# Two layers, forward and backward: the norm backward's last sum moved to VectorE, gradient copies halved, tail loads spread

## The chip, the cores and the metric

The kernel runs on one core of a Trainium2 chip. The metric is the device time of one execution in microseconds (us). Time before: 1142.19 us, the median of 3 runs (1139.85 to 1144.12).

The core's engines have the names that the profile gives them: PE is TensorE (matmul; PEld its weight load), DVE is VectorE, ACT is ScalarE, POOL is GpSimd, SP is SyncE, which here only issues transfers. "L860" is line 860 of the kernel file.

## The reference

Four residual layers are applied to x of 2048 x 512 in turn, attention (A), gated unit (B), A, B, with the same weights for both A and both B. The kernel returns the output and the gradients with respect to x and to all weights.

```python
def _layernorm(x, axis=-1, eps=1e-5):
    m = jnp.mean(x, axis=axis, keepdims=True)
    v = jnp.var(x, axis=axis, keepdims=True)
    return (x - m) / jnp.sqrt(v + eps)
# A: linear attention, 32 heads of 16
qkv = x @ wqkv                                    # 512 x 1536
pq, pk = phi(q), phi(k)                           # phi(t) = t+1 for t > 0, else exp(t)
kv, z = einsum(pk, v), sum(pk)
o = (pq @ kv) / (pq @ z)
A(x) = o @ wo                                     # 512 x 512
# B: F = 1376
B(x) = (sigmoid(x @ w_gate) * (x @ w_up)) @ w_down
# ... (cut: masks, shapes, small constants)
x = x + A(_layernorm(x)); x = x + B(_layernorm(x))
x = x + A(_layernorm(x)); x = x + B(_layernorm(x))
# outputs: x, and the vjp of it with grad_out for x, wqkv, wo, w_gate, w_up, w_down
```

The layers are numbered 0 (A), 1 (B), 2 (A), 3 (B). The backward goes 3, 2, 1, 0. Products are bfloat16, sums float32. The tokens are 16 tiles of 128 rows, in 4 blocks of 4 tiles (NB = 4, NBLK = 4); F is cut into 11 chunks of 128 (NFC = 11).

## The kernel before

Layer 3 is done forward and backward together; then `backward` runs layer 2 (`a_bwd`), layer 1 (`b_bwd`), layer 0 (`a_bwd`), and after these the gradients of the weights, for which activations and gradients that were stored before are loaded again, the latter transposed by the transfer.

Every tile of every layer goes through the backward of the norm. Its last line has two forms: one DVE operation, where `k.n_t` is 2 (layer 3), or a bias pass on ACT and a sum on POOL (layers 2, 1 and 0, where `k.n_t` is 4):

```python
def ln_bwd(k, l, st, dh_ps, h_st, up):
    nc = k.nc
    rstd = k.rstd[l][:, st:st + 1]
    c1 = k.small.tile([P, 1], F32, name="c1")
    c2 = k.small.tile([P, 1], F32, name="c2")
    t_sb = k.p_ln.tile([P, D], F32, name="t_sb", bufs=k.n_t)
    nc.scalar.activation(t_sb[:], dh_ps, ACT.Identity, scale=rstd, accum_out=c1[:])
    c1n = k.small.tile([P, 1], F32, name="c1n")
    nc.scalar.mul(c1n[:], c1[:], -1.0 / D)
    junk = k.p_ln.tile([P, D], BF16, name="junk", bufs=1)
    nc.vector.scalar_tensor_tensor(junk[:], t_sb[:], -1.0 / D, h_st, ALU.mult, ALU.mult, accum_out=c2[:])
    nc.vector.scalar_tensor_tensor(t_sb[:], h_st, c2[:], t_sb[:], ALU.mult, ALU.add)
    if k.n_t == 2:
        nc.vector.scalar_tensor_tensor(k.xs[st][:], t_sb[:], c1n[:], up, ALU.add, ALU.add)
    else:
        nc.scalar.activation(t_sb[:], t_sb[:], ACT.Identity, bias=c1n[:])
        nc.gpsimd.tensor_tensor(k.xs[st][:], t_sb[:], up, ALU.add)
```

Layer 1. A chunk is 4 matmuls into `dhh_ps`, a copy on ACT, a product `dd_t` on DVE, and 8 matmuls (`back`) that wait for `dd_t` and are queued two chunks later. At the end of a block, `back` starts the norm for four tiles:

```python
# ... (cut: b_bwd: pools with 4 buffers for dd_t, 2 for dhh_t)
        def back(b, fc, dd):

            if fc == 0:
                acc[b] = [k.ps2.tile([P, D], F32, name="dh_ps", tag="dwbank") for _ in range(NB)]
            for j in range(NB):
                for a in range(2):
                    nc.tensor.matmul(acc[b][j][:], lhsT=dd[:, a, rows(j)], rhs=(k.wuT, k.wgT)[a][:, fc, :],
                                     start=(fc == 0 and a == 0), stop=(fc == NFC - 1 and a == 1))
            if fc == NFC - 1:
                hst = k.p_h.tile([P, NB, D], BF16, name="hb_t", tag="h_t")
                nc.sync.dma_start(out=hst[:], in_=by_tile(sv["h"], b * NB, NB))
                for j in range(NB):
                    ln_bwd(k, l, b * NB + j, acc[b][j][:], hst[:, j, :], k.xs[b * NB + j][:])
# ... (cut: the sh_t loads)
            for f0, nf in FGRP:
                # ... (cut)
                for fc in range(f0, f0 + nf):
                    i = fc - f0
                    ps = k.ps.tile([P, SB], F32, name="dhh_ps", tag="bank")
                    mm4(k, ps[:], lambda c: k.wdT[:, c, FC0[fc]:FC0[fc] + P], lambda c: gTs[b][:, :, c, :])
                    dhh = p_g.tile([P, SB], BF16, name="dhh_t")
                    nc.scalar.mul(dhh[:], ps[:], 0.5)
                    dd = p_dd.tile([P, 2, SB], BF16, name="dd_t")
                    nc.vector.tensor_tensor(dd[:], dhh[:].unsqueeze(1).to_broadcast([P, 2, SB]), sh[:, i],
                                            ALU.mult)
                    late.append((b, fc, dd))
                    if fc < 4 if b == 0 else fc < 3:
                        k.fill.step(5 if b == 0 else 3)
                    store_dd(k, sv, b, fc, dd, nc.sync)
                    if len(late) > 2:
                        back(*late.pop(0))
                    if fc == 3 and b + 1 < NBLK:
                        grads(b + 1)
        while late:
            back(*late.pop(0))
```

Layers 2 and 0, first half. A block has four chunks dc; `a_grads` makes the bfloat16 copies of the next block's gradients (ACT), transposes them (PE) and copies these out of PSUM (ACT), all four tiles at chunk 1. `k.fill.step(n)` queues n matmuls of layer 3's w_down gradient, which have no other hurry. `soft` is queued two chunks late:

```python
def a_grads(k, b):
    nc = k.nc
    g_t = k.p_h.tile([P, NB, D], BF16, name="ga_t", tag="h_t")
    gT = k.p_hT.tile([P, NB, NDC, P], BF16, name="gaT_t", tag="hT_t")
    for j in range(NB):
        nc.scalar.copy(g_t[:, j, :], k.xs[b * NB + j][:])
        if j % 2 == 0:
            tp = k.ps.tile([P, 2 * NDC, P], BF16, name="T_ps", tag="bank")
        for c in range(NDC):
            nc.tensor.transpose(tp[:, j % 2 * NDC + c, :], g_t[:, j, c * P:(c + 1) * P], k.ident[:])
        if j % 2:
            nc.scalar.copy(gT[:, j - 1:j + 1].rearrange("p a c q -> p (a c) q"), tp[:])
    return g_t, gT
# ... (cut)
    grads = lambda b: gs.append(a_grads(k, b))

# ... (cut: sums: 16 matmuls into CT_ps)
    def soft(b, dc, dq, u_t, qp, rp, dqT):
        t_ps = k.ps.tile([P, SB], F32, name="t_ps", tag="bank")
        nc.tensor.matmul(t_ps[:], lhsT=k.bdmask[:], rhs=u_t[:], start=True, stop=True)
        w_t = ph1.tile([P, SB], BF16, name="w_t")
        nc.vector.scalar_tensor_tensor(w_t[:], t_ps[:], A["nz"][:, dc:dc + 1], dq[:], ALU.mult, ALU.add)
        nc.gpsimd.tensor_tensor(dqT[:, dc, :], w_t[:], rp[:, dc, :], ALU.mult)
        nc.vector.scalar_tensor_tensor(u_t[:], t_ps[:], -1.0, qp[:, dc, :], ALU.mult, ALU.mult,
                                       accum_out=dzp[:, dc, b:b + 1])
# ... (cut: loads of qr_l and qn_l for each block)
        for dc in range(NDC):
            ps = k.ps.tile([P, SB], F32, name="dq_ps", tag="bank")
            mm4(k, ps[:], lambda c: MT[:, c, dc * P:(dc + 1) * P], lambda c: gT[:, :, c, :])
            dq = ph1.tile([P, SB], BF16, name="dq_sb", bufs=3)
            k.mark = nc.scalar.copy(dq[:], ps[:])
            u_t = ph1.tile([P, SB], BF16, name="u_t", bufs=3)
            nc.vector.tensor_tensor(u_t[:], dq[:], qp[:, dc, :], ALU.mult)
            late.append((b, dc, dq, u_t, qp, rp, dqT))
            k.fill.step(2)
            if len(late) > 2:
                soft(*late.pop(0))
            if dc == 1 and b + 1 < NBLK:
                grads(b + 1)
        sums(b, g_t, qn)
```

Second half of these layers: `keys` writes `dkT_t` with DVE for the next block, from 16 matmuls in four PSUM banks `dpk_ps`; then 48 matmuls into `dh_ps`, and the norm's backward for the four tiles of the block.

The weight gradients. `joint(i, a)` is a job of 128 matmuls (`dw_cols`), a third of the columns of w_up or w_gate, over both B layers. `load_all` brings one stored tensor whole into SBUF, 4 transfers of 512 KB; its pool `dw_all` has two buffers, and `h2`, `h0` take those of `h3`, `h1`. `pieces` brings the other operand in parts of 4 tiles, most of them transposed by the transfer, through 6 buffers (`set_t`). All these transfers are issued by SP.

```python
        h3, h1 = load_all(k, sv[3]["h"], "h_all"), load_all(k, sv[1]["h"], "h_all")
        joint = lambda i, a: dw_cols(k, ("wu", "wg")[a], 0, SETS[i],
                                     [(h3, sv[3]["ddT"][a], sv[3]["ddN"][:, :, :, a]), (h1, sv[1]["ddT"][a])])
        k.p_dst = mpool("dw_stage", 6)
        joint(0, 0)
        mctx.close()
        k.p_set, k.p_dst = pool("dw_set_end", 6), pool("dw_stage_end", 6)
        k.p_sm = pool("dw_small", 2)
        for i, a in ((0, 1), (1, 0), (1, 1), (2, 0), (2, 1)):
            joint(i, a)
        p_all, k.p_all = k.p_all, pool("dw_all_end", 2)
        g1 = load_all(k, sv[1]["g"], "g_all")
        k.p_all = p_all
        h2, h0 = load_all(k, sv[2]["h"], "h_all"), load_all(k, sv[0]["h"], "h_all")
        for s in SETS:
            dw_rows(k, "wd", s, [(g1, sv[1]["hhT"])], sv[3]["wd"])
        for i, nm in ((1, "dkT"), (0, "dqT")):
            dw_cols(k, "wqkv", i * D, (0, D), [(h2, sv[2][nm]), (h0, sv[0][nm])])
            if i:
                dw_small(k)
```

```python
def put(k, ps, nm, rs, cs):

    r, w = ps.shape[0], ps.shape[1]
    new = k.p_dst.tile([P, D], BF16, name="dw_new")
    k.nc.scalar.copy(new[0:r, 0:w], ps)
    k.st.dma_start(out=k.outs[nm][rs, cs], in_=new[0:r, 0:w])
# ... (cut)
def dw_cols(k, nm, base, cols, srcs):

    c0, w = cols
    ps = dw_banks(k, NDC)
    for i, (h, src, *turned) in enumerate(srcs):
        for st, h_t, t in pieces(k, h, src, c0, w, *turned):
            for ic in range(NDC):
                k.nc.tensor.matmul(ps[ic][:, 0:w], lhsT=h_t[:, ic * P:(ic + 1) * P], rhs=t,
                                   start=(i == 0 and st == 0), stop=(i == len(srcs) - 1 and st == NST - 1))
    for ic in range(NDC):
        put(k, ps[ic][:, 0:w], nm, rows(ic), slice(base + c0, base + c0 + w))
# ... (cut: dw_rows, the same with g_all, adding the stored part of layer 3: part_l, L1203; sum on DVE, L1205)
```

## Time and profile before

| | us |
|---|---|
| time, median of 3 runs | 1142.19 (1139.85 to 1144.12) |
| profiled execution: span | 1140.3 |
| layer 2 backward | 525 to 643 |
| layer 1 backward | 643 to 769 |
| layer 0 backward, first half | 769 to 820 |
| layer 0 backward, second half | 820 to 890 |
| weight gradients | 890 to 1140 |

One line of a group in the page reads: line, engine, operation, out<-in, partitions x elements, count | busy us, mean ns of one | idle time of the engine just before them, and who ended most of it. Groups that the change touches:

```profile
L860 POOL TENSOR_TENSOR x<-t_sb,x 128x512 f32<-128x512 f32 x48 | 74.1, 1558 | 139.7 <-ACT c1n L852 115.8
L902 DVE TENSOR_TENSOR dd_t<-dhh_t,sh_t 128x1024 bf16<-128x1024 bf16 x44 | 33.7, 771 | 59.9 <-ACT dhh_t L900 54.5
L1185 PE MATMUL dw_ps<-set_t,h_all 128*128 128x512 bf16 (+1 forms) x1024 | 204.8, 362 | 1.4 <-ACT dw_new L1117 1.3
L1117 ACT CAST dw_new<-dw_ps 128x512 bf16<-128x512 f32 (+1 forms) x40 | 19.7, 573 | 219.8 <-PE dw_ps L1185 155.8
```

Matmuls are pipelined: 379 ns is the latency of one, and they start 0.216 us apart. A row of waits reads: engine, line, waited for whom: us in total, times, longest. A timeline row reads: start, duration, engine, line, operation, tiles, form, how many in a row, and the idle time before with who ended it.

### The profile page before, as it was taken

The numbers are of one execution on the slowest core, as the hardware profiler recorded it, in microseconds if no ns is written. First come the engines' busy times: TensorE is split into PE (matmuls) and PEld (weight loads), VectorE is DVE, ScalarE is ACT, GpSimd is POOL, SyncE is SP. The second block draws the span as 40 slices with busy tenths as digits, with TensorE's granted clock in tenths as the row PEclk, the third lists the DMA queues.
The fourth block names the chain that finished last, engine by engine and source line by source line (L and its number), as shares of the span: only waits on it lengthen the run. The fifth ranks groups of instructions, "written<-read, shape, count | busy, mean of one in ns | idle before, by whom it ended". The sixth has DMA issues, their size and how long they took to land.

```text
span 1140.3 us, 15748 instructions
## 1 busy us (share of the span) xinstructions
PE 1082.1 (95%) x5624; PEld 509.3 (45%) x5624; DVE 533.9 (47%) x951; ACT 506.8 (44%) x1034; POOL 381.7 (33%) x463
## 2 busy tenths in 40 slices
...
GB/s 258 256 235 239 264 244 244 182 181 245 285 231 106 236 78 250 89 266 247 271 282 212 191 232 247 219 182 308 336 182 95 191 275 172 136 216 250 228 231 115
DMA packets 376175, 248.13 MB, mean 218 GB/s; under 512 B 288784, under 2 KB 340528, under 8 KB 374304
## 3 DMA queue, kind: packets, MB, share of 16 engines
...
q8 instruction: 44, 0.72, 0.3%
...
## 4 chain that ended last, share of the span: by engine, by line
PE 20%; issue 20%; POOL 4%; DVE 4%; ACT 3%; DMA 3%; SPq 1%; POOLq 0%; DVEq 0%; ACTq 0%
PE dh_ps L879 5%; PE dhh_ps L180 2%; DVE junk L854 2%; PE fill_ps L236 2%; PE CT_ps L966 2%; POOL out_dram L1118 2%; PE dh_ps L790 2%; POOL x L860 2%; PE dh_ps L1037 2%; PE dq_ps L180 2%; DVE t_sb L855 1%; PE dh_ps L1098 1%; DMA qr_l<-sv_qr 1%; DMA pkT_l<-sv_pkT 1%; ACT t_sb L850 1%
## 5 line engine op out<-in xcount | busy, mean ns | idle before, releaser
L1185 PE MATMUL dw_ps<-set_t,h_all 128*128 128x512 bf16 (+1 forms) x1024 | 204.8, 362 | 1.4 <-ACT dw_new L1117 1.3
L651 POOL TENSOR_TENSOR sd_t<-sd_t,hh_t 128x512 bf16<-128x512 bf16 x88 | 107.8, 1236 | 121.6 <-DVE hh_t L649 89.2
L1185 PEld LDWEIGHTS <-h_all 128*128 128x128 bf16 x1024 | 100.2, 98 | 105.3 <-issue 1.9
L860 POOL TENSOR_TENSOR x<-t_sb,x 128x512 f32<-128x512 f32 x48 | 74.1, 1558 | 139.7 <-ACT c1n L852 115.8
L1117 ACT CAST dw_new<-dw_ps 128x512 bf16<-128x512 f32 (+1 forms) x40 | 19.7, 573 | 219.8 <-PE dw_ps L1185 155.8
L850 ACT ACTIVATE t_sb<-dh_ps,rstd 128x512 f32<-128x512 f32 x64 | 43.5, 680 | 127.7 <-PE dh_ps L790 93.4
L180 PE MATMUL g_ps<-hT_t,wg 128*128 128x512 bf16 x352 | 90.5, 379 | 6.9 <-DVE hh_t L649 3.7
L180 PE MATMUL u_ps<-hT_t,wu 128*128 128x512 bf16 x352 | 90.9, 380 | 0.6 <-DVE hh_t L649 0.6
L180 PE MATMUL dhh_ps<-gT_t,wdT 128*128 128x512 bf16 x352 | 91.2, 382 | 0.0
L1205 DVE TENSOR_TENSOR dw_new<-dw_ps,part_l 128x512 bf16<-128x512 f32 (+1 forms) x11 | 6.9, 684 | 179.7 <-PE dw_ps L1199 171.3
L1118 POOL DMA_DIRECT2D out_dram<-dw_new x40 | 21.4, 541 | 171.7 <-ACT dw_new L1117 170.3
L879 PE MATMUL dh_ps<-wuT,dd_t 128*128 128x512 bf16 x176 | 66.7, 379 | 3.8 <-DVE dd_t L902 3.7
L879 PE MATMUL dh_ps<-wgT,dd_t 128*128 128x512 bf16 x176 | 66.7, 379 | 0.0
L649 DVE SCALAR_TENSOR_TENSOR hh_t<-sd_t,u_ps 128x512 bf16<-128x512 bf16 x88 | 59.3, 679 | 14.1 <-ACT sd_t L648 13.5
L648 ACT ACTIVATE sd_t<-g_ps,onef 128x512 bf16<-128x512 f32 x88 | 60.8, 691 | 2.5
L902 DVE TENSOR_TENSOR dd_t<-dhh_t,sh_t 128x1024 bf16<-128x1024 bf16 x44 | 33.7, 771 | 59.9 <-ACT dhh_t L900 54.5
L650 ACT ACTIVATE sd_t<-g_ps,onef 128x512 bf16<-128x512 f32 x88 | 60.6, 689 | 0.0
L733 DVE TENSOR_TENSOR sd_t<-dhh_t,sd_t 128x1024 bf16<-128x1024 bf16 x44 | 30.4, 692 | 59.2 <-POOL sd_t L651 57.8
L647 ACT ACTIVATE g_ps<-g_ps 128x512 f32<-128x512 f32 x88 | 52.4, 602 | 8.8 <-PE g_ps L180 8.6
L180 PEld LDWEIGHTS <-wg 128*128 128x128 bf16 x352 | 33.9, 98 | 47.1 <-issue 8.8
L879 PEld LDWEIGHTS <-dd_t 128*128 128x128 bf16 x352 | 34.1, 98 | 46.4 <-DVE dd_t L902 5.8
L180 PEld LDWEIGHTS <-wu 128*128 128x128 bf16 x352 | 34.5, 98 | 42.3 <-issue 0.9
...
## 6 DMA issues: line engine op xcount, KB each, us to landing
...
```

The source lines that it names most:

```text
L180: i = k.nc.tensor.matmul(out, lhsT=lhs(c), rhs=rhs(c), start=(c == 0), stop=(c == n - 1))
L647: nc.scalar.activation(g_ps[:], g_ps[:], ACT.Tanh, scale=-0.5)
L648: nc.scalar.activation(sd[:, 0, :], g_ps[:], ACT.Identity, bias=k.onef[:], scale=-1.0)
L649: nc.vector.scalar_tensor_tensor(hh[:], sd[:, 0, :], 0.5, u_ps[:], ALU.mult, ALU.mult)
L650: nc.scalar.activation(sd[:, 1, :], g_ps[:], ACT.Identity, bias=k.onef[:])
L651: nc.gpsimd.tensor_tensor(sd[:, 1, :], sd[:, 1, :], hh[:], ALU.mult)
L850: nc.scalar.activation(t_sb[:], dh_ps, ACT.Identity, scale=rstd, accum_out=c1[:])
L860: nc.gpsimd.tensor_tensor(k.xs[st][:], t_sb[:], up, ALU.add)
L879: nc.tensor.matmul(acc[b][j][:], lhsT=dd[:, a, rows(j)], rhs=(k.wuT, k.wgT)[a][:, fc, :], start=(fc == 0 and a == 0), stop=(fc == NFC - 1 ...
L902: nc.vector.tensor_tensor(dd[:], dhh[:].unsqueeze(1).to_broadcast([P, 2, SB]), sh[:, i], ALU.mult)
L1118: k.st.dma_start(out=k.outs[nm][rs, cs], in_=new[0:r, 0:w])
L1185: k.nc.tensor.matmul(ps[ic][:, 0:w], lhsT=h_t[:, ic * P:(ic + 1) * P], rhs=t, start=(i == 0 and st == 0), stop=(i == len(srcs) - 1 and st ...
```

## The change

Five things change:

- `ln_bwd` asks `k.fused(st)` in place of `k.n_t == 2`. It is true for all tiles of layers 3 and 1, and for tiles with an even number in layers 2 and 0. There the last sum is one DVE operation in place of the ACT pass and the POOL sum; 16 of the 48 POOL sums stay. The number of `t_sb` buffers stays as it was.
- `a_grads` makes its copies in two halves of two tiles, at chunks 0 and 2 in place of all at chunk 1, so that less stands at once in the queues of ACT and PE.
- Layer 1 keeps a third chunk between `dd_t` and its matmuls, with a fifth `dd_t` buffer, so that PE may be later in asking for it.
- The loads of the tail are spread: `g_all` is asked for before the third pair of jobs, `h2` and `h0` after the first and the second part of the w_down gradient, in place of all three in one place, so that the transposes that PE needs sooner don't stand behind them.
- The last job goes through its last four tiles bank by bank, so that three of the four results are copied and stored while PE still works; these stores are issued by SP in place of POOL.

```diff
--- before.py
+++ after.py
@@ -706,7 +706,7 @@
     nc, sv = k.nc, k.sv[l]
     pool = lambda name, bufs: ctx.enter_context(k.tc.tile_pool(name=name, bufs=bufs))
     hhs, dds, gns, gTs = {}, {}, k.gns, k.gTs
-    k.n_t = 2
+    k.n_t, k.fused = 2, lambda st: True
 
     def down(b):
         for j in range(NB):
@@ -826,16 +826,21 @@
         mctx.close()
         k.p_set, k.p_dst = pool("dw_set_end", 6), pool("dw_stage_end", 6)
         k.p_sm = pool("dw_small", 2)
+        p_all, p_end = k.p_all, pool("dw_all_end", 2)
         for i, a in ((0, 1), (1, 0), (1, 1), (2, 0), (2, 1)):
+            if (i, a) == (2, 0):
+                k.p_all = p_end
+                g1 = load_all(k, sv[1]["g"], "g_all")
+                k.p_all = p_all
             joint(i, a)
-        p_all, k.p_all = k.p_all, pool("dw_all_end", 2)
-        g1 = load_all(k, sv[1]["g"], "g_all")
-        k.p_all = p_all
-        h2, h0 = load_all(k, sv[2]["h"], "h_all"), load_all(k, sv[0]["h"], "h_all")
-        for s in SETS:
+        for i, s in enumerate(SETS):
             dw_rows(k, "wd", s, [(g1, sv[1]["hhT"])], sv[3]["wd"])
+            if i == 0:
+                h2 = load_all(k, sv[2]["h"], "h_all")
+            elif i == 1:
+                h0 = load_all(k, sv[0]["h"], "h_all")
         for i, nm in ((1, "dkT"), (0, "dqT")):
-            dw_cols(k, "wqkv", i * D, (0, D), [(h2, sv[2][nm]), (h0, sv[0][nm])])
+            dw_cols(k, "wqkv", i * D, (0, D), [(h2, sv[2][nm]), (h0, sv[0][nm])], i == 0)
             if i:
                 dw_small(k)
 
@@ -853,7 +858,7 @@
     junk = k.p_ln.tile([P, D], BF16, name="junk", bufs=1)
     nc.vector.scalar_tensor_tensor(junk[:], t_sb[:], -1.0 / D, h_st, ALU.mult, ALU.mult, accum_out=c2[:])
     nc.vector.scalar_tensor_tensor(t_sb[:], h_st, c2[:], t_sb[:], ALU.mult, ALU.add)
-    if k.n_t == 2:
+    if k.fused(st):
         nc.vector.scalar_tensor_tensor(k.xs[st][:], t_sb[:], c1n[:], up, ALU.add, ALU.add)
     else:
         nc.scalar.activation(t_sb[:], t_sb[:], ACT.Identity, bias=c1n[:])
@@ -864,8 +869,9 @@
     nc, sv = k.nc, k.sv[l]
     with ExitStack() as ctx:
         p_g = ctx.enter_context(k.tc.tile_pool(name=f"bb_g{l}", bufs=2))
-        p_dd = ctx.enter_context(k.tc.tile_pool(name=f"bb_dd{l}", bufs=4))
+        p_dd = ctx.enter_context(k.tc.tile_pool(name=f"bb_dd{l}", bufs=5))
         gTs, acc, late = {}, {}, []
+        k.fused = lambda st: True
 
         def grads(b):
             gTs[b] = b_grads(k, l, b)
@@ -905,7 +911,7 @@
                     if fc < 4 if b == 0 else fc < 3:
                         k.fill.step(5 if b == 0 else 3)
                     store_dd(k, sv, b, fc, dd, nc.sync)
-                    if len(late) > 2:
+                    if len(late) > 3:
                         back(*late.pop(0))
                     if fc == 3 and b + 1 < NBLK:
                         grads(b + 1)
@@ -922,11 +928,13 @@
         a_bwd2(k, l, final, big, pool, CT, dzp, dqTs)
 
 
-def a_grads(k, b):
+def a_grads(k, b, half=None):
     nc = k.nc
-    g_t = k.p_h.tile([P, NB, D], BF16, name="ga_t", tag="h_t")
-    gT = k.p_hT.tile([P, NB, NDC, P], BF16, name="gaT_t", tag="hT_t")
-    for j in range(NB):
+    if half in (None, 0):
+        k.ga = (k.p_h.tile([P, NB, D], BF16, name="ga_t", tag="h_t"),
+                k.p_hT.tile([P, NB, NDC, P], BF16, name="gaT_t", tag="hT_t"))
+    g_t, gT = k.ga
+    for j in range(NB) if half is None else range(2 * half, 2 * half + 2):
         nc.scalar.copy(g_t[:, j, :], k.xs[b * NB + j][:])
         if j % 2 == 0:
             tp = k.ps.tile([P, 2 * NDC, P], BF16, name="T_ps", tag="bank")
@@ -957,8 +965,6 @@
     dzp = big.tile([P, NDC, NBLK], F32, name="dzp")
     CT_ps = [k.ps2.tile([P, D], F32, name="CT_ps", tag="dwbank") for _ in range(NDC)]
     late, gs, dqTs = [], [k.early], []
-
-    grads = lambda b: gs.append(a_grads(k, b))
 
     def sums(b, g_t, qn):
         for jc in range(NDC):
@@ -1003,8 +1009,10 @@
             k.fill.step(2)
             if len(late) > 2:
                 soft(*late.pop(0))
-            if dc == 1 and b + 1 < NBLK:
-                grads(b + 1)
+            if dc in (0, 2) and b + 1 < NBLK:
+                g = a_grads(k, b + 1, dc // 2)
+                if dc:
+                    gs.append(g)
         sums(b, g_t, qn)
     while late:
         soft(*late.pop(0))
@@ -1020,6 +1028,7 @@
 def a_bwd2(k, l, final, big, pool, CT, dzp, dqTs):
     nc, sv = k.nc, k.sv[l]
     p_dph, p_o = pool("ab_dph", 1), pool("ab_o", 1)
+    k.fused = lambda st: st % 2 == 0
 
     def loads(b):
         hT = k.p_hT.tile([P, NB, NDC, P], BF16, name="haT_l", tag="hT_t")
@@ -1110,12 +1119,12 @@
 
 
 
-def put(k, ps, nm, rs, cs):
+def put(k, ps, nm, rs, cs, eng=None):
 
     r, w = ps.shape[0], ps.shape[1]
     new = k.p_dst.tile([P, D], BF16, name="dw_new")
     k.nc.scalar.copy(new[0:r, 0:w], ps)
-    k.st.dma_start(out=k.outs[nm][rs, cs], in_=new[0:r, 0:w])
+    (eng or k.st).dma_start(out=k.outs[nm][rs, cs], in_=new[0:r, 0:w])
 
 
 def dw_small(k):
@@ -1175,17 +1184,26 @@
     return [pool.tile([P, D], F32, name="dw_ps", tag=tag) for _ in range(n)]
 
 
-def dw_cols(k, nm, base, cols, srcs):
+def dw_cols(k, nm, base, cols, srcs, last=False):
 
     c0, w = cols
     ps = dw_banks(k, NDC)
+    n, got = len(srcs) * NST, []
     for i, (h, src, *turned) in enumerate(srcs):
         for st, h_t, t in pieces(k, h, src, c0, w, *turned):
+            got.append((i * NST + st, h_t, t))
+            if last and n - NB <= got[-1][0] < n - 1:
+                continue
             for ic in range(NDC):
-                k.nc.tensor.matmul(ps[ic][:, 0:w], lhsT=h_t[:, ic * P:(ic + 1) * P], rhs=t,
-                                   start=(i == 0 and st == 0), stop=(i == len(srcs) - 1 and st == NST - 1))
-    for ic in range(NDC):
-        put(k, ps[ic][:, 0:w], nm, rows(ic), slice(base + c0, base + c0 + w))
+                for m, h_m, t_m in got:
+                    k.nc.tensor.matmul(ps[ic][:, 0:w], lhsT=h_m[:, ic * P:(ic + 1) * P], rhs=t_m,
+                                       start=(m == 0), stop=(m == n - 1))
+                if last and got[-1][0] == n - 1:
+                    put(k, ps[ic][:, 0:w], nm, rows(ic), slice(base + c0, base + c0 + w), k.nc.sync)
+            got = []
+    if not last:
+        for ic in range(NDC):
+            put(k, ps[ic][:, 0:w], nm, rows(ic), slice(base + c0, base + c0 + w))
 
 
 def dw_rows(k, nm, cols, srcs, part):
```

## The prediction

> **What bounds the kernel now.** I read the engine totals first, then the waits of TensorE by stretch, then the timelines of the stretches in which it waits.
>
> ```profile
> PE 1082.1 (95%) x5624; PEld 509.3 (45%) x5624; DVE 533.9 (47%) x951; ACT 506.8 (44%) x1034; POOL 381.7 (33%) x463
> ```
>
> TensorE (PE) is busy in 1082.1 of 1140.3 us; its matmuls stay. So the change can win idle time of PE and time in which PE runs slowly, no more: 58 us in all. The forward part, up to about 525 us, keeps its instructions in the same order on every engine; its share of the idle time (some 30 us) stays. Behind 525 us these are the waits, from the waits of PE in five stretches (us in total, times, longest):
>
> ```profile
> PE fill_ps L236 <- DVE dkT_t L1050: 1.7, 1, 1.7
> PE dq_ps L180 <- ACT dq_sb L999: 1.5, 1, 1.5
> PE dpk_ps L180 <- DVE dkT_t L1050: 1.1, 1, 1.1
> ...
> PE dh_ps L879 <- DVE dd_t L902: 3.7, 3, 1.6
> ...
> PE dq_ps L180 <- ACT dq_sb L999: 2.0, 2, 1.2
> PE T_ps L934 <- ACT dq_sb L999: 1.7, 1, 1.7
> PE T_ps L934 <- DVE u_t L975: 0.6, 1, 0.6
> ...
> PE dh_ps L1037 <- ACT t_sb L850: 1.0, 2, 0.6
> ...
> PE dw_ps L1199 <- DMA set_t<-sv_hhT: 5.0, 1, 5.0
> PE dw_ps L1185 <- ACT dw_new L1117: 1.3, 1, 1.3
> ```
>
> In order: layer 2 of the backward (525 to 643 us), layer 1 (643 to 769), the first half of layer 0 (769 to 820), its second half (820 to 890), the weight gradients (888 to 1141). The sum is near 22 us; about 20 us with the end of the program is all that the change could win, and 2% of 1142 is 22.8.
>
> Why layer 1 waits is in VectorE's (DVE) timeline at a block's end, with GpSimd (POOL) beside it (start, duration):
>
> ```profile
> 677.49 0.68 DVE L854 SCALAR_TENSOR_TENSOR junk<-t_sb,hb_t 128x512 bf16<-128x512 f32 x1
> 678.10 0.08 DVE L854 DVE_READ_ACCUMULATOR junk<-t_sb,hb_t 128x1 f32 x1
> 678.28 1.57 DVE L855 SCALAR_TENSOR_TENSOR t_sb<-hb_t,c,t_sb 128x512 f32<-128x512 bf16 x1
> 679.77 1.76 DVE L854 SCALAR_TENSOR_TENSOR junk<-t_sb,hb_t 128x512 bf16<-128x512 f32 x1
> 681.46 0.08 DVE L854 DVE_READ_ACCUMULATOR junk<-t_sb,hb_t 128x1 f32 x1
> 681.46 1.74 DVE L902 TENSOR_TENSOR dd_t<-dhh_t,sh_t 128x1024 bf16<-128x1024 bf16 x1
> ...
> 677.46 5.19 POOL L860 TENSOR_TENSOR x<-t_sb,x 128x512 f32<-128x512 f32 x3 [26.39 <-ACT c1n L852]
> ```
>
> While POOL adds x (5.19 us for three), the same DVE operations take 1.57 to 1.76 us that take 0.68 to 0.75 without it, and `dd_t`, for which PE waits, is one of them.
>
> The weight gradients show the longest wait, and what it drags behind it (PE, then the transfers that SyncE, SP, issued):
>
> ```profile
> 1027.89 13.98 PE L1199 MATMUL dw_ps<-g_all,set_t 128*128 128x512 bf16 x64
> 1046.87 27.31 PE L1199 MATMUL dw_ps<-g_all,set_t 128*128 128x512 bf16 x112 [5.00 <-DMA set_t<-sv_hhT]
> ...
> 1018.54 2.06 SPq L1152 DMA_DIRECT2D h_all<-sv_h  x4
> 1020.65 12.90 SPq L1166 DMA_TRANSPOSE set_t<-sv_hhT  x3
> 1033.64 2.35 SPq L1152 DMA_DIRECT2D h_all<-sv_h  x4
> 1036.03 15.94 SPq L1166 DMA_TRANSPOSE set_t<-sv_hhT  x4
> ```
>
> Two blocks of loads of 2 MB (4 times 512 KB) stand ahead of transposes that PE needs sooner. And 112 matmuls take 27.31 us, where at the pace of the 64 before (13.98 us, 0.216 us each) they would take 24.2: PE restarts slowly (granted clock 0.51 between 1046.5 and 1053 us). The wait costs 5.0 + 3.1 = 8.1 us.
>
> **What the Trainium skill says.** "SBUF — State Buffer", Who interferes with whom: a VectorE instruction with two SBUF inputs and a GpSimd one that reads SBUF exclude one another for a whole instruction. The lines above agree (0.7 us becomes 1.6 to 1.8). "TensorE: Matmul & The Clock Gate", What's actually happening: after an idle window of about 3.4 us the array falls to half its clock until it has been busy as long. The trace agrees for 5.0 us of idle time; waits of 1.7 us left the clock at 1.00. "DMA: Bandwidth & Descriptors", Issuing engines are not separate DMA queues: all transfers share 16 engines. The mean busy share of these is 1.14 from 1011 to 1054 us, so a load moved behind a transpose gives the transpose time that someone later pays.
>
> **The change part by part.**
>
> Last sum of the norm's backward on DVE. 32 of 48 sums leave POOL (all 16 of layer 1, every second one of layers 2 and 0), and with each a bias pass on ScalarE (0.72 us). DVE gains 32 operations; that form takes 0.75 us in the forward's last stage (L857), so 24 us on an engine busy 47%. In layer 1 a block's end then costs DVE 4 x (0.69 + 0.08 + 0.75 + 0.75) = 9.1 us, nothing stretched. In the changed program's order 4 `junk`, 4 `t_sb` and 3 sums stand ahead of the first late `dd_t`: 8.3 us, where before it was 674.55 to 681.46, 6.9 us, and then a `dd_t` of 1.74. So `dd_t` would be ready after 9.0 in place of 8.65 us.
>
> Third chunk in flight. A chunk on PE is 4 + 8 matmuls, 2.59 us; PE asks for each `dd_t` one chunk later. The lateness was 1.57, 1.57 and 0.59 us, plus 0.4 at most: under 2.59. All three waits go: **-3.7 us**. The fifth `dd_t` buffer is what lets it.
>
> Start of layer 0. PE waits 1.7 + 0.9 + 0.2 there because ScalarE has a bias pass in its queue that waits for DVE ahead of the copies of `dq_sb`. Those passes are gone. But DVE still ends layer 1: from its first `junk` at 768.04, four times 1.47 and three sums of 0.67 (starts to starts) put it at 776.0, and `u_t` at 776.5, while PE, with nothing else to wait for, asks for it at 768.26 + 6.9 = 775.2. So 2.8 us become about 1.3: **-1.5 us**. Gradient copies in halves: of the 1.0 us of small waits around transposes and copies (0.65 and three times 0.16, one of them counted above), **-0.7**. The waits of 1.5 and 1.2 us for `dq_sb` stand behind the load of `qr_l` (7.8 and 7.4 us in the chain) and stay.
>
> Second halves of layers 2 and 0. Waits for `dkT_t` (1.7 + 1.1) stay: the first of these sits behind one sum more (0.75) and one stretched `junk` fewer (1.0). Waits for `t_sb` (1.0) go with the shorter ScalarE queue; I take **-0.7**.
>
> Tail loads. In the changed order three of the four transposes of each group stand ahead of most of a load block. `g_all` doesn't move: it is issued at the same place in SP's order as before. The load blocks land at 1.5 us a piece, so without the second block the transpose that PE waited for comes 6 us earlier, at 1040.9, before 1041.7 when PE asks: the wait of 8.1 us goes. But the third group's first transpose was issued at 1054.11 and landed 5.4 us later (median), at 1059.5, behind just the same transfers as it will be; PE will ask for it at 1027.89 + 2 x 13.8 = 1055.5. So 0 to 4 us of waiting come back there, more with the slow clock if it exceeds about 3.4. I take 3 us and 0.6 for the clock: **-4.5 us**.
>
> Last job bank by bank. The four copies ran one after another from 1134.07 to 1136.12, and the last of the stores on POOL was issued at 1136.5. Now the last copy alone follows the last matmul (1134.6 to 1135.2), and its store goes out on SP: 1.2 us sooner, with a little less to issue: **-1.5 us**.
>
> Sum: 3.7 + 1.5 + 0.7 + 0.7 + 4.5 + 1.5 = 12.6; 1142.2 - 12.6 = 1129.6 us.
>
> **Rivals.** (1) The transfers bound the tail: the wait moves whole to the third group, with a second slow restart, and the tail gives 1 us, total 1133. For it: a DMA share over 1 from 1011 to 1120 us. Against: from 1054 to 1088 SP waits for buffers that PE frees for 12 us (4.5 + 3.9 + 3.8 in its waits), so the transfers have room later. (2) No wait comes back, the transposes run at the 2.1 us that the fastest show: tail -8, total 1126. (3) VectorE becomes the bound at layer borders: nine microseconds without a gap at each block's end, and the sums ahead of `dkT_t`; 3 to 5 us lost again, total 1134. Against: it is idle more than a third of every stretch. (4) The removed POOL work counts for more than the waits: then PE would have to be held elsewhere by POOL, and it is not; POOL appears in no wait of PE.
>
> **Range and chances.** The parts outside the tail are small and each read from its own wait: 8 us, give or take 3. The tail is 1 to 8. Together 1121 to 1138. Faster by 2% needs 1119.3, nearly every wait behind 525 us: 6%. Slower by 2% needs 23 us of new waits: 1%.
>
> **What would show it.** Right: no wait for `dd_t` in layer 1; its DVE operations at 0.7 us throughout; the first group's wait of 5.0 us gone, and a wait of 1 to 4 us on `hhT` one group later; a last store on SP. Wrong: a wait at layer 0's start above 2 us; waits for `dkT_t` grown past 4 us; a wait on `dkT` or `dqT` transposes; a clock under 0.9 in the tail twice.

## The result and the profile after

| | before | after |
|---|---|---|
| time, median | 1142.7 us (1139.85 to 1144.12) | 1133.26 us (1132.46 to 1136.54) |
| profiled execution: span | 1140.3 us | 1134.6 us |

The ratio is 0.9926, with a 95% interval of 0.9897 to 0.9954: 0.7% faster. The prediction was 1129.6 us with a range of 1121 to 1138, and the measured time lies in it; but 12.6 us were expected, and 8.5 (by the ratio) to 9.4 (by the medians) came. The first rival (the wait in the tail moves whole, 1133 us) named the number that was measured.

Busy time by engine in the profile after:

```profile
PE 1074.8 (95%) x5529; PEld 509.6 (45%) x5624; DVE 529.1 (47%) x983; ACT 487.7 (43%) x1002; POOL 324.5 (29%) x427
```

POOL lost 57 us of work and ACT 19 (before: 381.7 and 506.8), DVE 5 us (before: 533.9) although it makes 32 operations more: the others run faster. In layer 1, from its first `dhh_ps` to its last `dh_ps`, 14 of 89 VectorE operations took over 0.8 us before, and 1 of 103 does after. The PE count is lower only because records of matmuls are missing in this trace; the weight loads, 5624, are all there.

Two groups of the changed lines, from the page (line, engine, operation, out<-in, form, count | busy us, mean ns | idle time before and its cause):

```profile
L1199 PE MATMUL dw_ps<-set_t,h_all 128*128 128x512 bf16 (+1 forms) x1008 | 203.9, 362 | 2.5 <-ACT dw_new L1126 1.7
...
L908 DVE TENSOR_TENSOR dd_t<-dhh_t,sh_t 128x1024 bf16<-128x1024 bf16 x44 | 29.9, 690 | 58.7 <-ACT dhh_t L906 48.1
```

`dd_t` is at 690 ns on average, before 771. The sum that stays on POOL, from the groups of POOL (16 in place of 48; before 74.1 us):

```profile
L865 POOL TENSOR_TENSOR x<-t_sb,x 128x512 f32<-128x512 f32 x16 | 21.6, 1348 | 70.7 <-ACT t_sb L864 70.7
```

The waits of PE by stretch: layer 2 (525 to 643 us), then layer 0's first half (767 to 818), then the weight gradients (878 to 1134). For layer 1 and for the second half of layer 0 the view lists no wait.

```profile
PE dq_ps L180 <- ACT dq_sb L1005: 3.5, 1, 3.5
...
PE t_ps L977 <- DVE u_t L981: 3.2, 1, 3.2
PE dq_ps L180 <- ACT dq_sb L1005: 3.0, 1, 3.0
...
PE dw_ps L1217 <- DMA set_t<-sv_hhT: 4.2, 1, 4.2
PE dw_ps L1199 <- ACT dw_new L1126: 1.7, 2, 1.2
```

What the change was to remove is gone in this trace: `dd_t` (3.7), most of `dkT_t` (2.8) and `t_sb` in the second halves. In its place stand waits of 3.5 us in the first half of layer 2 and of 3.2 and 3.0 us in that of layer 0, where those for `dq_sb` and `u_t` were 1.5 and 4.3 in all, and 4.2 us for `hhT` where there were 5.0.

VectorE at a block's end in layer 1, in the timeline of the changed kernel (start, duration):

```profile
678.94 0.69 DVE L859 SCALAR_TENSOR_TENSOR junk<-t_sb,hb_t 128x512 bf16<-128x512 f32 x1 [0.57 <-ACT t_sb L855]
...
684.83 0.75 DVE L862 SCALAR_TENSOR_TENSOR x<-t_sb,c1n,x 128x512 f32<-128x512 f32 x1
685.49 0.74 DVE L860 SCALAR_TENSOR_TENSOR t_sb<-hb_t,c,t_sb 128x512 f32<-128x512 bf16 x1
686.15 0.68 DVE L908 TENSOR_TENSOR dd_t<-dhh_t,sh_t 128x1024 bf16<-128x1024 bf16 x1
```

Nothing here takes over 0.75 us, and the first late `dd_t` is done 7.9 us after the first `junk`, where the prediction had counted 9.0 and the kernel before took 8.65.

The tail, PE's timeline and then SyncE's transfers (issue, time to issue):

```profile
1026.26 27.79 PE L1217 MATMUL dw_ps<-g_all,set_t 128*128 128x512 bf16 x125
1058.24 12.22 PE L1217 MATMUL dw_ps<-g_all,set_t 128*128 128x512 bf16 x47 [4.20 <-DMA set_t<-sv_hhT]
```

```profile
1026.55 1.72 SPq L1161 DMA_DIRECT2D h_all<-sv_h  x3
1028.37 11.81 SPq L1175 DMA_TRANSPOSE set_t<-sv_hhT  x3
1040.22 0.57 SPq L1161 DMA_DIRECT2D h_all<-sv_h  x1
1040.89 5.01 SPq L1175 DMA_TRANSPOSE set_t<-sv_hhT  x1
1045.95 1.68 SPq L1161 DMA_DIRECT2D h_all<-sv_h  x3
1047.73 1.87 SPq L1221 DMA_DIRECT2D part_l<-sv_wd  x4
1050.26 12.05 SPq L1175 DMA_TRANSPOSE set_t<-sv_hhT  x4
```

The second group no longer waits. The third does, 4.2 us from 1054.04 on, for the transpose that was issued at 1050.26 and landed at 1058.20, behind all of `h2`, `h0` and four `part_l`.

**Where it went, stage by stage.** I divided each traced execution at the same matmuls: the last `dh_ps<-sd_t` (end of layer 3), the last `CT_ps`, the first `dhh_ps`, the last `dh_ps<-dd_t`, the last `CT_ps`, the last `dh_ps`, the first of the w_down gradient, the first of the `dkT` job, the last matmul, the end of the program. In us, each from one traced execution. The 2.8 us of `fill_ps` that open layer 0 are counted in its first half here; some of the expectations below leave them out (they start at the first `dq_ps`). The joint jobs before the w_down gradient take 148.9 us in every row; they and the last jobs are left out:

| kernel | layer 2, first half | second | layer 1 | layer 0, first half | second | w_down gradient | last matmul to end |
|---|---|---|---|---|---|---|---|
| before | 46.6 | 70.1 | 129.3 | 48.8 | 62.1 | 46.1 | 5.7 |
| e12, before + tail loads | 46.4 | 70.8 | 128.9 | 53.1 | 61.9 | 43.5 | 5.7 |
| e4, before + third chunk | 47.0 | 70.2 | 124.8 | 50.6 | 63.3 | 41.2 | 5.7 |
| e3, before + sum on DVE | 46.5 | 68.5 | 126.8 | 47.3 | 62.2 | 45.4 | 6.1 |
| after | 49.9 | 67.6 | 124.9 | 50.7 | 60.0 | 44.0 | 3.4 |
| after, once more | 46.3 | 70.4 | 124.9 | 50.6 | 60.6 | 43.7 | 3.4 |
| e1, after, h_all held | 49.9 | 67.6 | 124.8 | 48.0 | 61.8 | 42.3 | 3.4 |
| e11, after, haT_l and pkT_l held | 48.6 | 71.9 | 124.9 | 49.2 | 61.3 | 45.2 | 3.4 |
| e6, after, last stores on POOL | 46.7 | 70.4 | 125.8 | 48.8 | 60.0 | 45.5 | 5.0 |
| e5, after without halves | 46.9 | 68.2 | 124.8 | 50.3 | 62.5 | 45.6 | 3.3 |
| e2, after + early h2 | 50.4 | 67.8 | 124.8 | 49.1 | 60.0 | 38.0 | 3.4 |
| e9, e5 + early h2 | 46.6 | 69.2 | 124.8 | 49.2 | 61.7 | 38.0 | 3.3 |
| e13, e9 + h1 held | 47.6 | 72.1 | 126.0 | 46.7 | 72.3 | 38.0 | 3.4 |
| e14, e9 + all sums on DVE | 46.5 | 68.8 | 124.8 | 50.2 | 60.9 | 38.0 | 3.4 |

Before to after, in the two traces: layers 2 to 0 from 356.9 to 353.0 us (-3.9), w_down gradient -2.1, last matmuls +0.3, end -2.3; and +2.3 in the forward part, whose instructions have the same order in both. That is chance: in the second trace of the changed kernel the forward part is 2.6 us shorter than before. Together -5.7, the difference of the spans. The traced execution is the slowest of the changed kernel's four (1136.54 us), so some 3 to 4 us of the gain in the medians are in no stage of these two traces. That a stage may differ by over 3 us between two executions of the same kernel (layer 2, after and after once more) has to be kept in mind for every row.

### The profile page after: what moved, and what is told of

It is laid out like the page before. It is cut to its first block, busy times and chain, and to the rows that moved or that the text cites. A ratio compares the mean times of both kernels' runs of the same rounds, so it can differ in the third digit from the quotient of the medians.

```text
span 1134.6 us, 15573 instructions
## 1 busy us (share of the span) xinstructions
PE 1074.8 (95%) x5529; PEld 509.6 (45%) x5624; DVE 529.1 (47%) x983; ACT 487.7 (43%) x1002; POOL 324.5 (29%) x427
## 4 chain that ended last, share of the span: by engine, by line
PE 26%; issue 20%; POOL 4%; DMA 3%; DVE 2%; ACT 1%; POOLq 0%; SPq 0%; DVEq 0%; ACTq 0%
PE dh_ps L885 7%; PE dhh_ps L180 3%; PE fill_ps L236 3%; DMA qr_l<-sv_qr 2%; PE dw_ps L1199 2%; PE dh_ps L790 2%; PE dq_ps L180 2%; PE dh_ps L1107 2%; PE CT_ps L972 2%; PE dh_ps L1046 1%; POOL out_dram L1127 1%; PE dpk_ps L180 1%; POOL x L865 1%; PE y_ps L180 1%; POOL out_dram L1224 1%
## 5 line engine op out<-in xcount | busy, mean ns | idle before, releaser
L651 POOL TENSOR_TENSOR sd_t<-sd_t,hh_t 128x512 bf16<-128x512 bf16 x88 | 105.5, 1208 | 120.0 <-DVE hh_t L649 89.2
L855 ACT ACTIVATE t_sb<-dh_ps,rstd 128x512 f32<-128x512 f32 x64 | 43.5, 680 | 133.3 <-PE dh_ps L790 94.8
L885 PE MATMUL dh_ps<-wgT,dd_t 128*128 128x512 bf16 x170 | 64.4, 379 | 0.2
L650 ACT ACTIVATE sd_t<-g_ps,onef 128x512 bf16<-128x512 f32 x88 | 60.6, 688 | 0.0
L908 DVE TENSOR_TENSOR dd_t<-dhh_t,sh_t 128x1024 bf16<-128x1024 bf16 x44 | 29.9, 690 | 58.7 <-ACT dhh_t L906 48.1
L180 PEld LDWEIGHTS <-wu 128*128 128x128 bf16 x352 | 34.4, 98 | 42.3 <-issue 0.9
L790 PEld LDWEIGHTS <-sd_t 128*128 128x128 bf16 x352 | 34.5, 98 | 41.5
```

Of the source, the lines that this page charges most:

```text
L180: i = k.nc.tensor.matmul(out, lhsT=lhs(c), rhs=rhs(c), start=(c == 0), stop=(c == n - 1))
L650: nc.scalar.activation(sd[:, 1, :], g_ps[:], ACT.Identity, bias=k.onef[:])
L651: nc.gpsimd.tensor_tensor(sd[:, 1, :], sd[:, 1, :], hh[:], ALU.mult)
L790: k.nc.tensor.matmul(dh_ps[:], lhsT=dds[fc][:, a, rows(j)], rhs=(k.wuT, k.wgT)[a][:, fc, :], start=(i == 0), stop=(i == 2 * NFC - 1))
```

## The experiments

The times, each with the ratio to the kernel before on the same chip and its 95% interval. The kernel before had medians of 1144.25 us beside e1 to e4, 1146.35 beside e5, e9, e11 and the changed kernel again, and 1142.6 beside e12 to e14, so across these groups the ratios are to be compared and not the times:

| run | time, median us | ratio | interval |
|---|---|---|---|
| e12 tail loads alone | 1142.42 | 0.9996 | 0.9976 to 1.0015 |
| e4 third chunk alone | 1139.33 | 0.9959 | 0.9941 to 0.9977 |
| e3 sum alone | 1136.03 | 0.9915 | 0.9887 to 0.9942 |
| changed kernel again | 1134.52 | 0.9910 | 0.9877 to 0.9942 |
| e11 halves, loads held | 1140.03 | 0.9945 | 0.9925 to 0.9966 |
| e5 no halves | 1135.41 | 0.9904 | 0.9878 to 0.9930 |
| e1 h_all held | 1134.09 | 0.9907 | 0.9879 to 0.9935 |
| e2 early h2 | 1129.11 | 0.9881 | 0.9833 to 0.9928 |
| e9 no halves, early h2 | 1128.34 | 0.9864 | 0.9826 to 0.9903 |
| e13 e9 and h1 held | 1130.97 | 0.9903 | 0.9869 to 0.9937 |
| e14 e9 and all sums on DVE | 1126.33 | 0.9852 | 0.9820 to 0.9884 |

### The sum on VectorE alone (e3)

```diff
--- before.py
+++ e3
@@ forward and backward of layer 3 @@
-    k.n_t = 2
+    k.n_t, k.fused = 2, lambda st: True
@@ ln_bwd @@
-    if k.n_t == 2:
+    if k.fused(st):
@@ b_bwd @@
+        k.fused = lambda st: True
@@ a_bwd2 @@
+    k.fused = lambda st: st % 2 == 0
```

> The kernel before, with the norm's last sum on VectorE and nothing else changed (all tiles of layer 1, every second tile of layers 2 and 0; two chunks in flight in layer 1, four dd_t buffers). Theory (the sum takes POOL's stretching away but adds its own 0.75 us ahead of dd_t): layer 1 keeps three waits for dd_t of 1 to 2 us each, 3.5 to 5.5 us in all; the waits for dkT_t in layer 2's second half fall from 2.8 us to under 0.6; the whole kernel 0 to 3 us faster than before. Rival (the sum alone is what freed layer 1): no wait for dd_t above 0.5 us, layer 1 about 4 us shorter.

Measured: a ratio of 0.9915, some 8 to 10 us, where I had expected 0 to 3. It can't be told from the ratio of the whole change. The waits of PE in layer 1:

```profile
PE dh_ps L880 <- DVE dd_t L903: 1.4, 4, 0.4
```

My theory had 3.5 to 5.5 us here and fell; the rival had no wait over 0.5, which is what there is, but layer 1 is 2.5 us shorter (129.3 to 126.8), not 4. Without POOL beside it VectorE's chain to the first late `dd_t` takes 7.9 us with its added sums, and took 8.65 before without them:

```profile
672.74 0.69 DVE L854 SCALAR_TENSOR_TENSOR junk<-t_sb,hb_t 128x512 bf16<-128x512 f32 x1 [0.57 <-ACT t_sb L850]
...
679.95 0.69 DVE L903 TENSOR_TENSOR dd_t<-dhh_t,sh_t 128x1024 bf16<-128x1024 bf16 x1
```

The waits for `dkT_t` in layer 2's second half are 1.2 us; the kernel before has 2.8, and I had expected under 0.6:

```profile
PE fill_ps L236 <- DVE dkT_t L1052: 1.0, 1, 1.0
PE dpk_ps L180 <- DVE dkT_t L1052: 0.2, 1, 0.2
```

### The third chunk alone (e4)

```diff
--- before.py
+++ e4
-        p_dd = ctx.enter_context(k.tc.tile_pool(name=f"bb_dd{l}", bufs=4))
+        p_dd = ctx.enter_context(k.tc.tile_pool(name=f"bb_dd{l}", bufs=5))
...
-                    if len(late) > 2:
+                    if len(late) > 3:
                         back(*late.pop(0))
```

> The kernel before, with a third chunk in flight and a fifth dd_t buffer in layer 1 and nothing else changed (POOL still makes all its sums). Theory (a chunk of 2.6 us covers a lateness of 0.6 to 1.6 us whatever VectorE suffers from POOL): no wait for dd_t, layer 1 about 3.5 us shorter, VectorE operations still 1.6 to 1.8 us beside POOL, the start of layer 0 takes back 0 to 3.5 us of it as its qr_l loads land no sooner; the whole kernel 1 to 3 us faster than before. Rival (the third chunk only moves the wait to the block's border or needs the fused sum): waits of 2 us or more remain in layer 1.

Measured: no wait in layer 1, which falls to 124.8 us (4.5 less; with the sum on VectorE beside it, 124.8 to 126.0), although VectorE runs as slowly as before beside POOL. Its timeline at the same block's end:

```profile
679.45 1.57 DVE L855 SCALAR_TENSOR_TENSOR t_sb<-hb_t,c,t_sb 128x512 f32<-128x512 bf16 x1
680.94 1.76 DVE L854 SCALAR_TENSOR_TENSOR junk<-t_sb,hb_t 128x512 bf16<-128x512 f32 x1
682.63 0.08 DVE L854 DVE_READ_ACCUMULATOR junk<-t_sb,hb_t 128x1 f32 x1
682.63 1.75 DVE L902 TENSOR_TENSOR dd_t<-dhh_t,sh_t 128x1024 bf16<-128x1024 bf16 x1
```

So one more chunk of 2.6 us in flight covers the lateness though its cause stays, and either part alone takes most of the waits in layer 1: the two gains don't add up. Layer 0's first half is 50.6 us here and 47.3 in e3. On top of the sum, the third chunk takes 2.0 us off layer 1 (126.8 to 124.8), and the first half of layer 0 is longer in its turn: 49.2 to 50.3 in e5, e9 and e14, where e3 has 47.3. The ratio of 0.9959 (4.7 us) is somewhat above the 1 to 3 us expected.

### What holds layer 0's first half (e1 and e13)

In both kernels 4 MB of `h_all` for the weight gradients are asked for at layer 0's start. `qr_l` of block 2 lands at 797.34 us before and at 796.60 after, of block 3 at 808.86 and 809.37, though PE arrives 1.4 us sooner: about half of the gain of layer 1 is left at block 2, and none at block 3. The transfers of 768 to 818 us (KB each, median us from issue to landing), before and then after:

```profile
h_all<-sv_h SPq DMA_DIRECT2D x8, 512.0 KB, 6.5
qr_l<-sv_qr SPq DMA_DIRECT2D x2, 1024.0 KB, 7.6
```

```profile
h_all<-sv_h SPq DMA_DIRECT2D x7, 512.0 KB, 8.4
qr_l<-sv_qr SPq DMA_DIRECT2D x2, 1024.0 KB, 9.3
```

Experiment e1 holds all of `h_all` until layer 0's second half:

```diff
--- after.py
+++ e1
-        h3, h1 = load_all(k, sv[3]["h"], "h_all"), load_all(k, sv[1]["h"], "h_all")
+        h3, h1 = (load_all(k, sv[l]["h"], "h_all", k.ct_done) for l in (3, 1))
@@ end of a_bwd1 @@
-        nc.scalar.copy(CT[:, jc, :], CT_ps[jc][:])
+        k.ct_done = nc.scalar.copy(CT[:, jc, :], CT_ps[jc][:])
@@ load_all: each of its four transfers may start only after `first` @@
+        if first is not None:
+            held(k, first, ld)
```

> The changed kernel, but the 4 MB of h_all loads for the weight gradients (h3, h1) may start only after the last copy of CT of layer 0, that is in its second half, in place of at its first half's start. Theory (the first half of layer 0 is bound by its transfers, so that qr_l of blocks 2 and 3 lands at the same moment however early TensorE arrives): the two qr_l loads land in under 6 us in place of 8 to 10, TensorE's waits in the first half of layer 0 fall from 6.6 us to under 3, and that half is 3 to 5 us shorter; the whole kernel 2 to 5 us faster than the changed one (about 1129 to 1131 us, ratio to the kernel before about 0.989), less if the loads now disturb the second half. Rival (the waits come from the gradient copies in halves, which put ScalarE and PSUM in another order): the qr_l loads land sooner, but the waits stay within 1 us of 6.6 and the half stays 50.7 us long.

Measured: of the three waits in the first half (6.6 us) one of 3.7 is left, for `qr_l` of block 3; block 2's lands 5.9 us after its issue (10.3 in the changed kernel) and is waited for no more (0.3 us); block 3's takes 7.5, where I had expected under 6. The half is 2.7 us shorter. The two halves in one view (columns: us, then busy us and instructions of PE, PEld, DVE, ACT, POOL, then granted clock, DMA share, GB/s), the changed kernel and then e1:

```profile
768.00:818.00 50.00, 43.13 (x229) 20.74 (x231) 31.86 (x72) 23.16 (x42) 20.95 (x20) 1.00 1.06 318
818.00:878.00 60.00, 59.66 (x296) 28.03 (x300) 41.73 (x75) 27.30 (x68) 20.52 (x22) 1.00 0.54 160
```

```profile
768.00:818.00 50.00, 45.71 (x253) 22.39 (x256) 36.48 (x77) 24.23 (x44) 22.24 (x22) 1.00 0.75 238
818.00:878.00 60.00, 58.29 (x277) 26.56 (x280) 38.79 (x69) 25.59 (x62) 18.63 (x21) 1.00 0.69 226
```

PE gains 2.6 us in the first window and loses 1.4 in the second, where the held 4 MB now go out: 1.2 us are left. The mechanism is shown for block 2. Its yield is small, and the ratio of 0.9907 can't be told from the changed kernel's.

e13 holds only `h1`, half of these loads, in a kernel with early h2 and whole gradient copies (below):

```diff
--- e9
+++ e13
-        h3, h1 = load_all(k, sv[3]["h"], "h_all"), load_all(k, sv[1]["h"], "h_all")
+        h3, h1 = load_all(k, sv[3]["h"], "h_all"), load_all(k, sv[1]["h"], "h_all", k.ct_done)
@@ k.ct_done and load_all as in e1 @@
```

> The changed kernel with whole gradient copies and h2 early, and the load of h1 (2 MB of the 4 MB at the start of layer 0) held until the last CT copy of layer 0. Theory (layer 0's first half waits for qr_l of block 2, which lands behind 4 MB of h_all, and 2 MB less of these let it land 4 to 6 us sooner, while half the loads are few enough not to disturb the second half): the wait of 3.8 us for u_t falls under 1 us, the first half of layer 0 (from the last dh of layer 1) 47 us or less in place of 49.2, its second half within 1 us of 61.7; 2 us faster than without the hold, ratio to the kernel before about 0.984. Rival (transfers are the bound over the whole of layer 0): the second half gets longer by what the first gains, ratio 0.986.

Measured: the first half is 46.7 us, 2.5 less than without the hold, as expected (`qr_l` of block 2 lands 5.8 us after its issue, and nothing waits for `u_t`); the second is 72.3 us, 10.6 more, in the traced execution. SyncE's transfers, and the wait of PE behind them:

```profile
816.75 7.60 SPq L1157 DMA_DIRECT2D h_all<-sv_h  x4
824.45 0.55 SPq L1171 DMA_DIRECT2D set_t<-sv_ddN  x1
825.10 11.98 SPq L1173 DMA_TRANSPOSE set_t<-sv_ddT  x1
837.18 0.53 SPq L1031 DMA_DIRECT2D haT_l<-sv_hT  x1
```

```profile
847.20 3.17 PE L180 MATMUL dpk_ps<-haT_l,Wp_t 128*128 128x512 bf16 x7 [9.51 <-DMA haT_l<-sv_hT]
```

The held loads put a transpose behind them that occupies SyncE for 12 us, and `haT_l`, which the next block needs, is asked for only then. In e1 `haT_l` went out within the held loads, at 827.34. In these traces half the loads did more harm than all of them: the place in SyncE's order counts, not the bytes alone. But the traced execution is the slowest of the seven (1140.29 us, with a median of 1130.97), so the others can't all have had this wait. The theory fell, and the hold is not shown to pay (0.9903 beside e9's 0.9864; the intervals overlap).

### The gradient copies in halves (e5, e11, changed kernel again)

In the first trace of the changed kernel layer 2's first half was 3.3 us longer than before. Only the halves change anything there. They also move loads: SyncE asks for `haT_l` and, in layer 0, `pkT_l` ahead of a transpose and of `qr_l` of block 3.

```diff
--- after.py
+++ e5
-            if dc in (0, 2) and b + 1 < NBLK:
-                g = a_grads(k, b + 1, dc // 2)
-                if dc:
-                    gs.append(g)
+            if dc == 1 and b + 1 < NBLK:
+                gs.append(a_grads(k, b + 1))
```

> The changed kernel with the gradient copies whole again, all four tiles at chunk 1 as in the kernel before; everything else as changed. Theory A (the halves cost time in the first halves of layers 2 and 0: with them SyncE asks for haT_l, in layer 0 also for pkT_l and ahead of a transpose, before qr_l of block 3, so that qr_l lands later): layer 2's first half is 46.5 us in place of 49.9, its wait for dq_sb falls from 3.5 to 1.5 us; layer 0's first half is 44.5 to 46.5 us in place of 47.9; the whole kernel 4 to 6 us faster than the changed one, about 1128 us, ratio to the kernel before about 0.988. Theory B (layer 0's first half is bound by its transfers of h_all whatever the order): layer 2's first half shortens by 3.4 us, layer 0's stays within 0.7 us of 47.9. Rival (the halves have no part in it): both stay within 0.5 us of what they are.

e11 keeps the halves and puts the loads back:

```diff
--- after.py
+++ e11
+        if b == NBLK - 1:
+            k.mark3 = k.mark
@@ loads(b) in a_bwd2: lds are the transfers of haT_l and pkT_l @@
+        if b == 0:
+            held(k, k.mark3, *lds)
```

> The changed kernel with its halves, but the first haT_l and pkT_l of the second half of layers 2 and 0 may start only after the last dq_sb copy of block 2, so that SyncE asks for qr_l of block 3 before them. Theory A (it is the order of the loads that costs, not the halves on TensorE and ScalarE): qr_l of block 3 lands 6 to 7.5 us after its issue in place of 8.4 to 8.8, layer 2's first half is about 46.5 us in place of 49.9 and layer 0's 45 to 46.5 in place of 47.9, as without halves. Rival (the halves' own order on TensorE and ScalarE costs): qr_l lands sooner, but the two first halves stay over 49 and 47 us.

And the changed kernel once more:

> The changed kernel itself once more, beside the others on the same chip. Expected: ratio to the kernel before 0.990 to 0.994; its wait of 3 to 4.5 us for hhT in the third group of the tail, and the first halves of layers 2 and 0 at 49.9 and 47.9 us within 1 us. Rival (these were chance of one execution): either half within 1 us of the kernel before's 46.6 and 46.0.

Measured: e5 has 46.9 us in layer 2's first half, as theory B said, with 1.8 us of waiting for `dq_sb`; layer 0's stays (50.3). But the changed kernel's second trace has 46.3 us there, with the halves, and 70.4 in the second half in place of 67.6. Its waits in layer 2:

```profile
PE fill_ps L236 <- DVE dkT_t L1059: 2.9, 1, 2.9
PE dq_ps L180 <- ACT dq_sb L1005: 1.4, 1, 1.4
PE dpk_ps L180 <- DVE dkT_t L1059: 0.2, 1, 0.2
```

The same 3 us are waited in one half or in the other, and the other traces with the same layer 2 fall on the two sides. The changed kernel's first trace, e1 and e2 wait 3.5 to 3.6 us for `dq_sb` in the first half and at most 0.5 for `dkT_t` in the second; the changed kernel again and e6 wait 1.4 to 1.6 and 3.1. In the three `qr_l` of block 3 lands 8.8 to 8.9 us after its issue, in the two after 6.7 and 7.0; why it differs isn't shown. So the first half alone was no measure, and one trace couldn't show what the halves cost. The rest of the changed kernel's second trace is as expected: 50.6 us in layer 0's first half, and a wait of 3.8 us for `hhT` in the third group.

Over both halves of layer 2, the six traces with halves have a median of 117.5 us (116.7 to 120.4), the five with whole copies and sums on DVE 115.3 (115.0 to 119.7), the three with sums on POOL 117.2 (116.7 to 117.2). By these medians the sums gave layer 2 about 1.9 us and the halves took about 2.2; but one group alone spreads over up to 4.7 us, so neither is shown. In the sum of layer 0's halves the six have 110.2 (108.8 to 111.2), e5, e9 and e14 111.1 (110.8 to 112.8): a gain of 1. The times don't decide it (0.9904 without, 0.9910 and 0.9926 with).

In e11 `qr_l` of block 3 lands after 5.9 us in layer 0, and that first half is 46.4 us without `fill_ps` (49.2 with it), as theory A said; layer 2's is 48.6, between theory and rival. The kernel is slower all the same (0.9945). Why isn't shown: its second halves have waits of 2.7 us for `dkT_t` and 1.1 for `haT_l`, but such waits stand in other traces too (2.9 in the changed kernel again, 2.4 in e5). Whether the halves cost layer 2 two microseconds, and why, stays open.

### The tail (e12 and e2)

e12 is the kernel before with the three load blocks placed as in the change, and nothing else.

```diff
--- before.py
+++ e12
+        p_all, p_end = k.p_all, pool("dw_all_end", 2)
         for i, a in ((0, 1), (1, 0), (1, 1), (2, 0), (2, 1)):
+            if (i, a) == (2, 0):
+                k.p_all = p_end
+                g1 = load_all(k, sv[1]["g"], "g_all")
+                k.p_all = p_all
             joint(i, a)
-        p_all, k.p_all = k.p_all, pool("dw_all_end", 2)
-        g1 = load_all(k, sv[1]["g"], "g_all")
-        k.p_all = p_all
-        h2, h0 = load_all(k, sv[2]["h"], "h_all"), load_all(k, sv[0]["h"], "h_all")
-        for s in SETS:
+        for i, s in enumerate(SETS):
             dw_rows(k, "wd", s, [(g1, sv[1]["hhT"])], sv[3]["wd"])
+            if i == 0:
+                h2 = load_all(k, sv[2]["h"], "h_all")
+            elif i == 1:
+                h0 = load_all(k, sv[0]["h"], "h_all")
```

> The kernel before with the tail's loads spread as in the change and nothing else (g_all ahead of the third pair, h2 and h0 after the first and second part of the w_down gradient). Theory (the wait for hhT moves whole from the second group to the third, because the same transfers stand ahead of it one group later): from the first w_down matmul to the first dkT matmul 43 to 46 us as in the kernel before (46.1), with one wait of 3.5 to 5 us for hhT in the third group; ratio to the kernel before 0.998 to 1.001. Rival (the prediction's step: 4.5 us of 8.1 come off): that stretch at 41.6 us or less, ratio about 0.996.

Measured: 0.9996, no difference. PE's timeline shows why:

```profile
1035.72 27.79 PE L1204 MATMUL dw_ps<-g_all,set_t 128*128 128x512 bf16 x125
1067.18 12.16 PE L1204 MATMUL dw_ps<-g_all,set_t 128*128 128x512 bf16 x47 [3.67 <-DMA set_t<-sv_hhT]
```

The 176 matmuls of the w_down gradient take 38.0 us without a wait. With the loads as before (before, e3, e4) the stretch took 46.1, 45.4 and 41.2 us; with them spread and h2 late (after, again, e1, e5, e6, e11, e12) 42.3 to 45.6, with a median of 44.0. Spread alone, the loads cost about what they cost before, one group later.

e2 asks for `h2` with `g_all`, at 920 us, 140 us before its first use, into the second buffer of the pool `dw_all_end`, which stood empty:

```diff
--- after.py
+++ e2
-                g1 = load_all(k, sv[1]["g"], "g_all")
+                g1, h2 = load_all(k, sv[1]["g"], "g_all"), load_all(k, sv[2]["h"], "h_all")
                 k.p_all = p_all
...
-            if i == 0:
-                h2 = load_all(k, sv[2]["h"], "h_all")
-            elif i == 1:
+            if i == 1:
                 h0 = load_all(k, sv[0]["h"], "h_all")
```

> The changed kernel, but h2 is loaded beside g_all, into a second buffer that is free early, so that only h0 stands between the transposes of the tail. Theory (the third group waits 4.2 us for hhT and then loses about 1.7 us to a slow clock because 2 MB of h0 and its neighbours are ahead of it in the transfers): that wait goes or falls under 1 us, the tail is 5 to 6 us shorter, the whole kernel about 1128 us, ratio to the kernel before about 0.987. Rival (the transfers bound the tail as a whole): the wait moves to another place, such as the second pair of jobs beside which h2 now loads or the first dkT transpose, with over 3 us of waiting in one place, and the time stays within 2 us of the changed kernel's 1133.

Measured: 1129.11 us, and not one wait in the w_down gradient:

```profile
1022.50 38.15 PE L1215 MATMUL dw_ps<-g_all,set_t 128*128 128x512 bf16 x172
```

38.0 us from the first to the `dkT` job, in e9, e13 and e14 too; no wait takes its place in the jobs beside which `h2` now loads. The mean busy share of the DMA engines rises there, from 878 to 1020 us, from 0.83 to 0.91. So 2 MB less to transfer in the w_down gradient was the cure; a new order of the same transfers was none. The share of the DMA engines doesn't tell the two apart: from 1026 to 1080 us it is 1.10 to 1.18 in the changed kernel and 1.13 to 1.15 in e2.

### Both, and all sums on VectorE (e9, e14)

e9 is e2 with the diff of e5, and e14 adds:

```diff
--- e9
+++ e14
@@ a_bwd2 @@
-    k.fused = lambda st: st % 2 == 0
+    k.fused = lambda st: True
```

> The changed kernel with whole gradient copies and with h2 loaded early, both at once. Theory (the two losses lie in different stages and add up): 3.4 us in layer 2, 1.5 to 3 in layer 0 and 6 in the tail, about 1122 us, ratio to the kernel before about 0.982, faster than either alone. Rival (what is gained earlier is waited away in the tail, where transfers are short): not more than 2 us better than early h2 alone, which had 0.988.

> The changed kernel with whole gradient copies and h2 early, and the norm's last sum on VectorE for every tile of layers 2 and 0 too, in place of every second one. Theory (a sum left on POOL stretches VectorE operations by about 1 us and VectorE is not the bound): the second halves of layers 2 and 0 are 0.5 to 2 us shorter, waits for dkT_t of 1.7 us fall under 1 us; ratio to the kernel before 0.984 to 0.986. Rival (16 more sums of 0.75 us stand ahead of dkT_t on VectorE): waits for dkT_t grow to 3 us or more, the second halves 1 to 3 us longer, ratio 0.988.

Measured: 0.9864 and 0.9852, the two best. On one chip e9's median is 6.2 us below the changed kernel's and 7.1 below e5's; in the traces the w_down gradient is 7.6 us shorter in e9 than in e5. e9's theory of 0.982 lies just outside its interval, and its rival (not more than 2 us better than early h2 alone) fits: whether whole copies add anything to early h2 is not decided (0.9864 and 0.9881). With 16 more sums on VectorE no wait for it grew in the second halves: `dkT_t` makes PE wait 1.6 us, and 1.9 in e9. The theory had it fall under 1 us and the rival had it grow to 3.

Second halves of 68.8 and 60.9 us are 0.4 and 0.8 less than e9's, within what two executions differ by. So the choice of every second tile was not needed; that moving all sums is better isn't shown.

### The last stores (e6)

```diff
--- after.py
+++ e6
-                    put(k, ps[ic][:, 0:w], nm, rows(ic), slice(base + c0, base + c0 + w), k.nc.sync)
+                    put(k, ps[ic][:, 0:w], nm, rows(ic), slice(base + c0, base + c0 + w))
```

> The changed kernel with the last job's stores issued by POOL as before; the bank by bank order stays. Looked at: the stretch from the end of the last matmul to the end of the program, 5.66 us in the kernel before and 3.35 in the changed one. Theory (most of the 2.3 us comes from the last copy standing alone, 1.5 us of copies less): 3.6 to 4.4 us. Rival (the store's way through POOL is the most of it): 4.8 us or more.

Measured in one execution: 4.98 us from the last matmul to the end. So of the 2.3 us, 0.7 come from the copies bank by bank and 1.6 from the store's way over SyncE; the theory had them the other way round. The last store in e6, in POOL's timeline:

```profile
1133.38 0.54 POOL L1127 DMA_DIRECT2D out_dram<-dw_new  x1 [0.32 <-ACT dw_new L1126]
```

POOL's store lands 2.0 us after its issue, at 1135.35, and the program ends 2.1 us later; in the changed kernel SyncE's lands 1.7 us after its issue at 1131.93, at 1133.63, and the program ends 1.0 us later. So most of the 1.6 us lies after the landing. The kernel before and e12, whose last stores go through POOL too, end 1.6 us after theirs, so how much of the 2.1 us is POOL's stays open.

## Why the prediction was right, and where it was wrong

- **Layer 1, -3.7 for the waits.** Right: all are gone, and layer 1 is 4.4 us shorter. The step "So `dd_t` would be ready after 9.0 in place of 8.65 us", from which the third chunk was to save the gain, was wrong: the chain to `dd_t` became shorter (7.9 us), since I had added up full durations where starts follow closer on one another; the sum alone left 1.4 us of waits. Each of the two parts works alone (e3, e4).
- **Start of layer 0, -1.5.** Right in its place: about 1.3 us were to be left, and 0.4 are there. But that "the waits of 1.5 and 1.2 us for `dq_sb` stand behind the load of `qr_l`" and "stay" failed: a wait that stands behind a transfer grows by what is gained ahead of it, if the transfer comes no sooner. (At block 2 of layer 0 e3 waits 1.9 us for `u_t`; e5, whose layer 1 is 2.0 us shorter, waits 3.6.) The waits became 3.5 us in layer 2 (in three of five traces) and, in layer 0, 3.2 at block 2 and 3.0 at block 3; e1 and e13 show for block 2 that the loads of `h_all` were the cause.
- **Halves, -0.7.** Not found: by the medians of traces about -1 in layer 0 and +2 in layer 2, and nothing that the times show.
- **Second halves, -0.7, "waits for `dkT_t` stay".** Perhaps undersized: by the medians of traces the sums took about 1.9 us off layer 2. Whether the end of the stretching or the ACT passes that go did it, no run separates.
- **Tail, -4.5.** The step that failed by most. Its mechanism was right (the third group asks 27.78 us after the first matmul, its operand lands 31.94 after it; the prediction had 27.6 and 31.6), and "I take 3 us and 0.6 for the clock" was mis-sized: it was 4.2 and 1.7, for 48 matmuls took 12.06 us where the pace is 10.4. So the trace before lost 8.1 us and the one after 5.9, and the part alone gives 0.5 us, between a gain of 2.7 and a loss of 1.7 (e12). I had written the reason beside it: a load moved behind a transpose gives the transpose time that someone later pays. The Trainium skill, "DMA: Bandwidth & Descriptors", Issuing engines are not separate DMA queues, says that all transfers share 16 engines, whichever engine issues them. Here SyncE issues all of these, so the runs don't test the second half of that; that the loads delay the transposes is what e12 and e2 show (0.5 us for the new order, 6.0 in the trace for 2 MB taken out of the stretch).
- **Last job, -1.5.** It was 2.3. The copies, which the prediction put first, are 0.7 of it and the store's way over SyncE is 1.6 (e6).

The range was drawn wider than its parts: 8 us give or take 3 and a tail of 1 to 8 make 1123 to 1136, not 1121 to 1138.

Of the rivals, the first described what happened in the tail. The second fell, for the wait came back. The third did not come: with every sum on VectorE (e14) no wait for `dkT_t` grew. The fourth is not shown either: the waits that went were for VectorE's results, and POOL's work counted by what it did to VectorE. Taken together, e3 alone has the gain of the change in layers 2 to 0: 351.4 us, beside 353.0 and 352.8 in the two traces of the changed kernel. Third chunk and halves added nothing to it that can be measured. Of the rest, the end's 2.3 us are in both traces; the 2.1 us of the w_down gradient are no more than e12 leaves open.
